# Attention by blocks of queries through all heads, with the first dense products placed between its steps

## The chip, the core and the metric

The kernel runs on one core of one Trainium2 chip. The metric is the device time of one execution in microseconds (us). The engines named below are PE (TensorE; PEld is its weight load), DVE (VectorE), ACT (ScalarE), POOL (GpSimd) and SP (SyncE), which only starts DMAs here. Each engine executes its own instructions in the order in which the program emits them, and waits at an instruction until its operands are there.

## The reference: what is computed

Two batches of 768 positions go through three stages.

1. Attention with 8 heads of 64 columns. A query sees the 96 keys up to and including itself and the first 8 keys; a slope for each head times the distance is subtracted from the score. Softmax, then the product with the values.
2. A gated unit: `h = relu(x @ w_in)` with 512 inputs and 1024 outputs, cut into `u` and `v`; `v` is normalised over its columns, multiplied over the positions with `w_spatial` (768x768), a bias is added, and the product with `u` goes through `w_out`.
3. A mixing unit: a rank-32 product over positions (`U`, `V`) is added to `x`, and then `relu(u @ w_ch1) @ w_ch2` with 2048 hidden columns is added.

## The kernel before, in words

Attention works on blocks of 128 queries. A block sees at most 232 keys (96 before it, 8 global ones, its own 128); the first block of a batch sees only 128. The heads go in pairs. A unit is one pair and one block; there are 2 batches x 4 pairs x 6 blocks = 48 units. The loop in `attention()` runs over units, all blocks of one pair before the next pair. One unit is: two score matmuls (`em_s`, 64 contraction rows each), bias and row maximum on DVE (`em_soft`), exponential and row sum on ACT (`em_exp`), a reciprocal of the sums for three units at a time on DVE (`em_sums`), the scaling on POOL (`em_norm`), transposes on PE (`em_t`) five units later, their move out of PSUM on ACT or DVE (`em_pt`), and, for three units at once, the product with the values (`em_pv`), which leaves PSUM as a rounded part and a rest (`em_x`: ACT, then DVE). The scores have four PSUM banks, the transposes two, the output two.

The dense products take every operand as such a rounded part and a rest, and use three matmuls for one product (`mm3`). The names: `m1_v` is the product with the `v` half of `w_in` (for one batch 6 tiles x 4 x 3 = 72 matmuls of 512 columns), `m2` the product with `w_spatial` (144 matmuls of 384 columns for one batch), `m1_u` that with the `u` half (96 matmuls), `m3` that with `w_out`, `m4` and `m5` those of stage 3.

Some weights come as 64-bit numbers and are decoded on the chip (`decode`: one ACT and four DVE operations for 512 columns, and then one ACT operation for the rounded part and one POOL operation for the rest). Half of `w_in` has four such pieces. They pass through a staging tile `stg` with two halves (`staged`): the third piece's DMA can start only when the first piece has left its half.

What is emitted when: `Plan` holds a model of every engine's time. Side work (decoding, loads, the normalisation of `v`) is put in as chains of operations. `tick()`, called after nearly every step, emits an operation of a chain when the model has that engine free soon enough; a chain put in while `plan.calm` is set comes after the others. `flush()` emits what is left of some chains at once, at that place of the program.

The order of the program before: attention, during whose last third the pieces of the `v` half of `w_in` are decoded as calm chains; then `m1_v` for both batches, `m2` of batch 0, `m1_u` of batch 0, `m2` of batch 1, `m1_u` of batch 1, `m3` and the rank-32 steps, and stage 3. `w_spatial` and the `u` half are decoded during `m1_v`.

The lines that set this order, from the end of `attention()` and behind it:

```
                            if p == 2:
                                plan.calm = True
                                wins = win_work(1, 0, 2048)
                ...
                flush(wins)
        ...
        for b in range(B):
            for t in range(NB):
                m1_v(b, t, bank[t % 4])
```

## Time and profile before

| | us |
|---|---|
| three runs | 552.78, 552.86, 553.55 (median 552.86) |
| the profiled execution, its time | 553.45 |
| the profiled execution, its span | 551.7 |
| busy in the span: PE / PEld / DVE / ACT / POOL | 520.7 / 450.9 / 293.8 / 217.3 / 181.0 |

Mean granted TensorE clock: 0.984 of full speed. The span is the time from the first to the last instruction. Busy time is a union over the instructions of an engine. Matmuls are pipelined and their ends are modelled, so that a start is a better mark than an end. Rows of a timeline merge neighbouring instructions of one kind: start, length, engine, line, operation, output and input, count, and in brackets the idle time before it with what ended it. All of the kernel's own instructions carry the line of one helper (L58), so the names of the tiles tell them apart: `raw` is the tile of queries, keys and probabilities, `sm` one of small numbers, `win` is `w_in`, `wsp` is `w_spatial`, `vals` the values.

### The profile page before, as it was taken

To read this page: it belongs to the slowest core of one execution; us is meant where nothing else is said; L and a number is where in the kernel's file an instruction comes from. 1 tells how busy PE (TensorE), PEld (TensorE's weight loads), DVE (VectorE), ACT (ScalarE), POOL (GpSimd) and SP (SyncE) were. 2 spreads that over 40 slices of the span, in tenths; PEclk is the share of its full clock that TensorE was granted. 3 is DMA by queue.
4 is the path that set the end of the run, shared out by engine and by line. 5 is a ranking of instruction groups with operands and counts; after the bars stand their busy time and mean duration, and the time that the engine had idled before them with its cause. 6 is when DMAs were issued, how large, how long until landed. Compare 5 with 4: busy or idle time off the path is not lost.

```text
span 551.7 us, 8005 instructions
## 1 busy us (share of the span) xinstructions
PE 520.7 (94%) x2916; PEld 450.9 (82%) x2916; DVE 293.8 (53%) x701; ACT 217.3 (39%) x527; POOL 181.0 (33%) x207
## 2 busy tenths in 40 slices
PE   5988887499999999999999999999999999999995
PEld 3656665378899999988899889889899899899894
DVE  6675656547775962379689867767122111110113
ACT  4677778355441510355453343342221221221220
POOL 2553545274471500322013432332322322323310
PEclk9999999779999999999999999999999999999998
DMA  7344331442121210232204442440003000000003
GB/s 281 120 128 150 112 130 55 163 143 87 38 78 42 76 33 0 80 131 97 74 4 135 170 154 85 145 151 2 0 3 112 1 1 1 1 0 1 1 2 120
DMA packets 9504, 42.81 MB, mean 78 GB/s; under 512 B 1264, under 2 KB 1392, under 8 KB 7408
## 3 DMA queue, kind: packets, MB, share of 16 engines
q1 hardware_dynamic: 9312, 42.21, 22.5%
q8 instruction: 25, 0.41, 0.3%
q14 instruction: 23, 0.19, 0.1%
q10 hardware_dynamic: 144, 0.00, 0.0%
HBM read 39.06 MB, written 3.15 MB: 77 GB/s over the span
## 4 chain that ended last, share of the span: by engine, by line
PE 81%; DVE 6%; ACT 6%; DMA 2%; issue 2%; POOL 2%; ACTq 0%; DVEq 0%; POOLq 0%
PE bank L58 81%; ACT raw L58 5%; DVE prob L58 3%; DVE sm L58 1%; DMA stg<-in_w_in_dram 1%; ACT x L58 1%; POOL raw L58 1%; DMA ni<-in_gl_dram 1%; DVE x L58 1%; DVE y L58 1%; DVE stg L58 1%; POOL vn L58 0%; DVE bias L58 0%; POOL win L58 0%; ACT stg L58 0%
## 5 line engine op out<-in xcount | busy, mean ns | idle before, releaser
L58 POOL TENSOR_TENSOR wch<-f,wch 128x512 fp32r<-128x512 f32 x64 | 85.7, 1359 | 213.6 <-ACT wch L58 213.6
L58 PE MATMUL bank<-x,wch 128*128 128x384 f32 x768 | 139.4, 336 | 0.0
L58 PE MATMUL bank<-wch,h 128*128 128x512 f32 x576 | 139.2, 395 | 0.0
L58 PEld LDWEIGHTS bank<-x,wch 128*128 128x128 f32 x768 | 134.7, 188 | 3.0
L58 PEld LDWEIGHTS bank<-wch,h 128*128 128x128 f32 x576 | 107.6, 188 | 23.4
L58 DVE SCALAR_TENSOR_TENSOR h<-bank,h 128x384 fp32r<-128x384 f32 x64 | 35.5, 555 | 141.6 <-ACT h L58 141.6
L58 ACT ACTIVATE h<-bank 128x384 fp32r<-128x384 f32 x64 | 31.4, 491 | 179.0 <-PE bank L58 179.0
L58 POOL TENSOR_SCALAR raw<-raw,sm 128x232 f32<-128x232 f32 (+1 forms) x96 | 43.2, 470 | 51.2 <-DVE sm L58 49.7
L58 ACT ACTIVATE raw<-prob,sm 128x232 f32<-128x232 f32 (+1 forms) x96 | 44.5, 466 | 26.2 <-DVE sm L58 17.6
L58 PE MATMUL bank<-wsp,vn 128*128 128x384 f32 x288 | 50.4, 335 | 0.4 <-ACT work L58 0.4
L58 PEld LDWEIGHTS bank<-wsp,vn 128*128 128x128 f32 x288 | 49.9, 188 | 0.8 <-ACT work L58 0.8
L58 DVE TENSOR_SCALAR f<-f 128x512 f32<-128x512 f32 (+1 forms) x64 | 40.7, 672 | 10.0 <-ACT f L58 9.7
L58 PE MATMUL bank<-win,x 128*128 128x512 f32 x144 | 37.3, 421 | 7.5 <-ACT win L58 6.9
L58 DVE SCALAR_TENSOR_TENSOR f<-raw,f 128x512 int32<-128x512 int32 x64 | 43.8, 725 | 0.1
L58 PE MATMUL bank<-raw 64*128 64x232 f32 (+1 forms) x192 | 35.6, 435 | 6.9 <-DMA raw<-in_qk_dram 5.7
L58 PEld LDWEIGHTS bank<-win,x 128*128 128x128 f32 x144 | 28.8, 203 | 15.7 <-ACT win L58 7.4
L58 PE MATMUL bank<-ident,raw 128*128 128x128 f32 (+1 forms) x176 | 30.2, 290 | 9.7 <-ACT raw L58 8.5
L58 PEld LDWEIGHTS bank<-ident,raw 128*128 128x128 f32 (+1 forms) x176 | 18.7, 140 | 24.3 <-POOL raw L58 11.9
L58 ACT ACTIVATE wch<-f 128x512 fp32r<-128x512 f32 x64 | 36.8, 624 | 1.1 <-DVE f L58 1.1
L58 PE MATMUL bank<-wo,x 128*128 128x512 f32 x144 | 35.2, 394 | 0.0
L58 PE MATMUL bank<-x,win 128*128 128x384 f32 x192 | 34.0, 336 | 0.0
L58 PEld LDWEIGHTS bank<-x,win 128*128 128x128 f32 x192 | 33.6, 188 | 0.0
(84 smaller groups left out, 505.6 us busy)
## 6 DMA issues: line engine op xcount, KB each, us to landing
raw<-in_w_ch_dram SPq DMA_DIRECT2D x16, 1024.0 KB, 4.9
vals<-in_vab_dram SPq DMA_DIRECT2D x8, 704.0 KB, 4.1
raw<-in_qk_dram SPq DMA_DIRECT2D x7, 792.0 KB, 4.5
stg<-in_w_in_dram SPq DMA_DIRECT2D x8, 512.0 KB, 4.1
out_dram<-y SPq DMA_DIRECT2D x12, 256.0 KB, 2.3
stg<-in_w_out_dram SPq DMA_DIRECT2D x4, 512.0 KB, 3.8
stg<-in_w_sp_dram SPq DMA_DIRECT2D x2, 768.0 KB, 5.3
raw<-in_qk_dram SPq DMA_DIRECT2D x2, 396.0 KB, 5.3
```

What stands on the lines that cost most here:

```text
L58: return f(*a, **kw)
```

## The change

A step g of the attention is now one block of 128 queries of one batch through all four pairs (12 blocks, `NBL`), and the host lays out queries, keys and values by block. In step g the scores of block g, the product with the values of block g-2 and the transposes of block g-1 are emitted. The four pairs' scores share four banks, two pairs side by side in each bank; softmax and exponential work in place in seven probability tiles; the sums are inverted for two pairs at a time (`em_norm`).

Between the transposes of the pairs `fill()` emits steps from a list. A step is one `mm3` of three matmuls: four steps make a tile of `m1_v` of batch 0; 48 steps are `m2` of batch 0. In steps 3 to 8 one is emitted after each pair, in steps 10 to 13 three. The transposes have two banks up to step 8 and one after that; the fillers of `m1_v` have one bank, those of `m2` two.

The `v` half of `w_in` and then `w_spatial` are put in as chains, not calm, before the first step (`early_work`). Their tiles, and those of `v` and `m2`, are no longer shared with the attention's; the attention uses other tiles in their place, among them those of the `u` half of `w_in`, whose decoding therefore is put in after the attention (`later_places`, `wu`). Then come `m1_v` of batch 1, `m1_u` of batch 0, `m2` of batch 1 and the rest as before. `U` and `V` are put in one `m1_u` later. The reciprocal root of the variance is taken with shift, negation, scaling and three Newton steps on DVE in place of a root on ACT, a reciprocal and one step.

The core of the diff (lines of the old attention that fall away are those shown above):

```diff
+            def o_load(g, e):
+                c = 0 if g % NB else C1
+                return [o_dma(raw_qk[g % 2][:, 2 * e:2 * e + 2, c:],
+                              qk[g // NB, g % NB].rearrange("p (r c) -> p r c", r=NP)[:, 2 * e:2 * e + 2, c:])]
...
+            def score(r, h):
+                return bank[r // 2 * 2 + h][:, CW * (r % 2):CW * (r % 2) + CW]
+            def prob(g, r):
+                return pb[(NP * g + r) % 7]
...
+            def em_norm(g, e):
+                r_in = rin[:, e]
+                V.tensor_scalar(out=r_in, in0=sums[:, e], scalar1=1.0e-9, scalar2=None, op0=ALU.add)
+                V.reciprocal(out=r_in, in_=r_in)
+                for r in range(2 * e, 2 * e + 2):
                     for h in range(2):
...
+                        x = prob(g, r)[:, h, c0_(g):CW]
+                        G.tensor_scalar(out=x, in0=x, scalar1=rin[:, e, r % 2, h:h + 1], scalar2=1.0,
+                                        op0=ALU.mult, op1=ALU.mult)
+            TWO = 9
+            def em_t(g, r):
+                x, bk = prob(g, r), bank[7 if g < TWO and r % 2 else 4].rearrange("p (h c q) -> p h c q", h=2, c=2)
+                c = 0 if g % NB else 1
+                if not c:
...
                 make_identity(nc, ident)
+                loads = {1: [plan.add(o_load(1, e)) for e in range(2)]}
+                pvals = {0: [], 1: [plan.add(o_vals(1))]}
+                early_work()
...
+                for g in range(NBL + 2):
+                    more = 1 if g < TWO else 3
+                    if g == NB:
+                        second_x()
+                    xs = None
+                    if g < NBL:
+                        flush(loads.get(g, []))
+                        for r in range(NP):
+                            em_s(g, r)
+                        if 0 < g and g + 1 < NBL:
+                            loads[g + 1] = [plan.add(o_load(g + 1, e)) for e in range(2)]
+                        tick()
+                    if g >= 2:
+                        flush(pvals[g - 2])
+                        em_pv(g - 2)
+                        if g < NBL:
+                            pvals[g] = [plan.add(o_vals(g))]
+                        xs = em_x(g - 2)
+                    if g < NBL:
+                        if g == 0:
+                            for h in range(2, 4):
+                                o_bias(B0, d0, m1, h)[1]()
+                        em_soft(g, 0)
+                        em_exp(g, 0)
+                    if 0 < g <= NBL:
+                        em_norm(g - 1, 1)
+                    if g < NBL:
+                        em_soft(g, 1)
+                        em_exp(g, 1)
+                        if g == 0:
+                            for h in range(4, 8):
+                                o_bias(B0, d0, m1, h)[1]()
                     if xs:
                         xs[0]()
...
+                    for r in range(NP):
+                        if xs and r == 1:
+                            xs[1]()
+                        if 0 < g <= NBL:
+                            em_t(g - 1, r)
+                            tick()
+                        fill(more)
+                        if g < NBL:
+                            if r < 2:
+                                em_soft(g, 2 + r)
+                                em_exp(g, 2 + r)
+                            if r == 1:
+                                em_norm(g, 0)
                         tick()
...
+                    if g == 0:
+                        for h in range(H):
+                            o_bias(Bt, rel, mk, h)[1]()
+                        plan.add([("V", f) for f in o_counts() + o_flag()])
+                    if 2 <= g < NB + 2:
+                        fillers.extend(s_m1_v(0, g - 2, 6))
+                    if g == TWO:
+                        fillers.extend(s_m2(0, 6))
         else:
...
+        def fill(n):
+            while n and fillers:
+                fillers.pop(0)()
+                n -= 1
...
+        def early_work():
+            win_places(1)
+            P["wv"] = win_work(1, 0, 2048)
             t_ = tl(T_SP, N_SP, "wsp")
             P["wsp"] = [t_[:, l * NB * S:(l + 1) * NB * S].rearrange("p (s t) -> p s t", s=NB) for l in range(2)]
...
+            P["vn"] = [[tl(T_VN[0][l], N_VN, f"vn0{l}").rearrange("p (t f) -> p t f", t=NB) for l in range(2)]]
             u_ = tl(T_UT, N_UT, "u")
             P["ut"] = u_.rearrange("p (k t) -> p k t", k=KB)
...
+            P["ws"] = [staged(lambda t, c=c: make(t, c)) for c in range(0, NB * S, 1536)]
+        def later_places():
+            win_places(0)
+            P["vn"].append([tl(T_VN[1][l], N_VN, f"vn1{l}").rearrange("p (t f) -> p t f", t=NB) for l in range(2)])
+            P["vw"].append([w[:, DM * n:DM * n + DM] for w in (tl(T_WK, N_WK, "work0"), tl("uv", 2 * S, "work1"))
+                            for n in range(3)])
+        def s_m1_v(b, t, k0):
+            bk = bank[k0]
+            def step(k):
+                if (b, t, k) == (0, 0, 0):
+                    flush(P["wv"])
                 mm3(bk, [X[b][l][:, k, 128 * t:128 * t + 128] for l in range(2)],
                     [win[1, l][:, k] for l in range(2)], k == 0, k == KB - 1)
...
+                if k == KB - 1:
+                    vw = P["vw"][b][t]
+                    A.activation(out=vw, in_=bk, func=AF.Relu)
+                    V.bn_stats(out=st[:, t % 2], in_=vw)
+                    V.bn_aggr(out=mv[:, b, t], in_=st[:, t % 2])
+                    if t % 3 == 2:
+                        lns[b, t // 3] = ln(b, t // 3)
+                tick()
...
+        def s_m2(b, k0):
+            def step(j, f, s, bk):
+                if (b, j, f, s) == (0, 0, 0, 0):
+                    flush(P["ws"] + [P["bs"]])
+                if j == 0 and f == 0 and s % 3 == 0:
+                    flush(lns[b, s // 3])
+                if b and j == 1 and f == 0 and s == 0:
+                    flush(gs[1])
+                c, e = 384 * j, 384 * j + 384
+                mm3(bk[:, 0:384], [P["vn"][b][l][:, s, 128 * f:128 * f + 128] for l in range(2)],
+                    [P["wsp"][l][:, s, c:e] for l in range(2)], s == 0, s == NB - 1)
+                if s == NB - 1:
+                    V.tensor_tensor(out=P["ut"][:, f, c:e], in0=bk[:, 0:384], in1=bsp[:, c:e], op=ALU.add)
+                tick()
+            return [lambda j=j, f=f, s=s: step(j, f, s, bank[k0 + f % 2 if k0 else f])
+                    for j in range(2) for f in range(KB) for s in range(NB)]
...
+        lns, gs = {}, []
+        attention()
+        later_places()
         wu = win_work(0, 0, 2048)
...
+        fill(1000)
+        for t in range(NB):
+            fillers.extend(s_m1_v(1, t, t % 4))
+        fill(1000)
         P["wo"] = [tl(f"win1{l}", 2048, f"wo{l}").rearrange("p (k f) -> p k f", k=KB) for l in range(2)]
...
                 gs.append(gated(b, j))
             if b == 0:
...
+                flush(lns[1, 0] + lns[1, 1])
+                w = tl("uv", 2 * S, "uvk")
+                upk, vpk = w[:, 0:S].rearrange("p (s r) -> p s r", s=NB), w[:, S:2 * S]
+                P["upk"], P["vpk"] = upk, vpk
+                uv = [staged(make_u), staged(lambda t: make_v(t, 0)), staged(lambda t: make_v(t, 384))]
+                fillers.extend(s_m2(1, 0))
+                fill(1000)
         P["raw"] = [tl(f"win0{l}", 2048, f"raw{l}") for l in range(2)]
         flush(gs[2] + gs[3])
         flush(w_o + uv)
```

## Rows read from the trace of the kernel before

**Rows 1.** Windows: us, busy (xcount) of PE, PEld, DVE, ACT, POOL, PEclk, DMA share, GB/s.

```profile
49.10:97.20 48.10, 41.49 (x391) 28.29 (x390) 31.14 (x144) 35.97 (x126) 24.19 (x54) 1.00 0.30 102
97.20:111.40 14.20, 6.74 (x52) 5.18 (x51) 7.63 (x14) 5.46 (x10) 4.28 (x4) 0.74 0.48 158
120.00:130.00 10.00, 10.00 (x45) 8.26 (x45) 7.72 (x17) 6.63 (x12) 5.59 (x4) 1.00 0.36 105
171.60:540.00 368.40, 368.40 (x1888) 335.21 (x1887) 179.43 (x300) 118.40 (x229) 100.33 (x76) 1.00 0.17 56
```

**Rows 2.** Timeline of PE from the attention's end to the u half's product.

```profile
101.30 1.85 PE L58 MATMUL bank<-win,x 128*128 128x512 f32 x6
110.07 0.79 PE L58 MATMUL bank<-win,x 128*128 128x512 f32 x1 [6.92 <-ACT win L58]
111.41 34.67 PE L58 MATMUL bank<-win,x 128*128 128x512 f32 x137 [0.55 <-POOL win L58]
146.48 25.26 PE L58 MATMUL bank<-wsp,vn 128*128 128x384 f32 x144 [0.40 <-ACT work L58]
171.58 16.83 PE L58 MATMUL bank<-x,win 128*128 128x384 f32 x96
```

**Rows 3.** Timeline of SP, the same columns: the third and fourth piece's DMAs.

```profile
98.72 1.65 SPq L58 DMA_DIRECT2D stg<-in_w_in_dram  x2
```

**Rows 4.** Timeline of PE within the attention, units in a row without idle time.

```profile
20.38 0.66 PE L58 MATMUL bank<-raw 64*128 64x232 f32 x4
20.98 0.64 PE L58 MATMUL bank<-ident,raw 128*104 128x128 f32 x4
21.55 1.32 PE L58 MATMUL bank<-raw,vals 128*64 128x128 f32 x20
22.80 0.66 PE L58 MATMUL bank<-raw 64*128 64x232 f32 x4
23.39 0.44 PE L58 MATMUL bank<-ident,raw 128*128 128x128 f32 x2
...
92.23 1.54 PE L58 MATMUL bank<-raw,vals 104*64 104x128 f32 x24
```

**Rows 5.** Waits from 8 to 97.2 us: us in total, times, longest.

```profile
DVE sm L58 <- ACT raw L58: 28.6, 16, 2.2
```

**Rows 6.** Timeline of DVE within the attention.

```profile
87.01 0.52 DVE L58 TENSOR_TENSOR x<-bank,x 128x384 fp32r<-128x384 f32 x1
87.44 0.39 DVE L58 CUSTOM_DVE_ANT_0 prob<-bank,bias 128x232 f32<-128x232 f32 x1
...
88.71 0.69 DVE L58 COPY raw<-bank 128x512 f32<-128x512 f32 x1
89.31 0.39 DVE L58 CUSTOM_DVE_ANT_0 prob<-bank,bias 128x232 f32<-128x232 f32 x1
```

**Rows 7.** Groups of ACT from 8 to 97.2 us: busy us, mean ns, idle before.

```profile
L58 ACT ACTIVATE raw<-prob,sm 128x232 f32<-128x232 f32 x80 | 38.2, 480 | 10.5 <-DVE sm L58 10.5
```

**Rows 8.** Groups of DVE over the whole span, the decoding in the staging tile.

```profile
L58 DVE SCALAR_TENSOR_TENSOR stg<-stg 128x512 int32<-128x512 int32 (+2 forms) x30 | 22.0, 746 | 0.2
...
L58 DVE TENSOR_SCALAR stg<-stg 128x512 f32<-128x512 f32 (+5 forms) x30 | 13.1, 460 | 4.2 <-ACT stg L58 4.1
```

**Rows 9.** Timeline of DVE at the start.

```profile
7.73 0.28 DVE L58 CUSTOM_DVE_ANT_0 prob<-bank,bias 128x128 f32<-128x128 f32 x1
...
7.94 0.70 DVE L58 SCALAR_TENSOR_TENSOR bias<-raw 128x232 f32<-128x232 f32 x2
```

**Rows 10.** Timeline of POOL: the scaling of three units, twice.

```profile
87.26 2.45 POOL L58 TENSOR_SCALAR raw<-raw,sm 128x128 f32<-128x128 f32 x6 [2.72 <-DVE sm L58]
92.71 3.90 POOL L58 TENSOR_SCALAR raw<-raw,sm 128x232 f32<-128x232 f32 x6 [3.00 <-DVE sm L58]
```

**Rows 11.** DMA issues: KB each, median us to landing.

```profile
raw<-in_qk_dram SPq DMA_DIRECT2D x7, 792.0 KB, 4.5
stg<-in_w_in_dram SPq DMA_DIRECT2D x8, 512.0 KB, 4.1
```

More of the change, by code (lines that the diff above doesn't have):

```diff
@@ L26 @@
 CW = C1 + 128
-KST = 128 + GS
-KXW = NB * KST
-VP = 22 * D
-QKW = KST + 128
+QKW = CW + 128
+NBL = B * NB
 NCH = 16
@@ L368, in stt @@
+            t_ = tl("x10", KB * S, "masks")
+            rel, mk = (t_[:, k * CW:(k + 1) * CW] for k in range(2))
+            iot = t_[:, 512:512 + CW + 128].bitcast(I32)
+            ps0, r0, d0, m1 = (t_[:, 1024 + 128 * k:1152 + 128 * k] for k in range(4))
             def stt(o_, i0, sc, i1, op0, op1):
@@ new lines, in em_soft, with em_exp @@
+            def em_soft(g, r):
+                c0, bt = c0_(g), Bt if g % NB else B0
+                for h in range(2):
+                    V.tensor_tensor_reduce(out=prob(g, r)[:, h, c0:CW], in0=score(r, h)[:, c0:CW], in1=bt[:, 2 * r + h],
+                                           scale=-0.125, scalar=3.0e38, op0=ALU.add, op1=ALU.min,
+                                           accum_out=mneg[:, (NP * g + r) % 8, h:h + 1])
+            def em_exp(g, r):
+                for h in range(2):
+                    x = prob(g, r)[:, h, c0_(g):CW]
+                    A.activation(out=x, in_=x, func=AF.Exp, scale=-1.0, bias=mneg[:, (NP * g + r) % 8, h:h + 1],
+                                 accum_out=sums[:, r // 2, r % 2, h:h + 1])
@@ new lines, in body @@
+            TWO = 9
+            def em_t(g, r):
+                x, bk = prob(g, r), bank[7 if g < TWO and r % 2 else 4].rearrange("p (h c q) -> p h c q", h=2, c=2)
+                c = 0 if g % NB else 1
+                if not c:
+                    for h in range(2):
+                        T.transpose(bk[0:C1, h, 0], x[:, h, 0:C1], ident)
+                for h in range(2):
+                    T.transpose(bk[:, h, 1], x[:, h, C1:CW], ident)
+                if r % 2:
+                    V.tensor_copy(ptb[r][:, :, c:], bk[:, :, c:])
@@ L484, in em_pt @@
                 else:
[L485 removed]
+                    A.activation(out=ptb[r][:, :, c:], in_=bk[:, :, c:], func=AF.Copy)
             def em_pv(g):
[L489 to L493 removed]
+                for r in range(NP):
+                    for c in range(0 if g % NB else 1, 2):
+                        k = (C1, 128)[c]
@@ L494, in em_pv @@
                         for h in range(2):
-                            T.matmul(bank[5 + g % 2][64 * h:64 * h + 64, 128 * (u % 3):128 * (u % 3) + 128], w[0:k, n, h],
-                                     ptb[u % 6][0:k, h, c], start=c == 0 or not i, stop=c == 1)
+                            T.matmul(bank[5][64 * h:64 * h + 64, 128 * r:128 * r + 128], vt[g % 2][0:k, r, c, h],
+                                     ptb[r][0:k, h, c], start=c == 0 or g % NB == 0, stop=c == 1)
             def em_x(g):
-                b, pr, i = units[3 * g]
@@ L567, in attention @@
-                flush(wins)
-                return lambda: None, []
+                    for r in range(NP):
+                        if xs and r == 1:
[10 more added lines that the diff above has]
+                                em_norm(g, 0)
+                        tick()
@@ L643, in attention @@
                                 sub(V, lo, bank[5][:, 0:128], hi)
-                flush(win_work(1, 0, 2048))
-                return lambda: None, []
-        P = {}
+                early_work()
+                for b in range(1):
+                    for t in range(NB):
+                        fillers.extend(s_m1_v(0, t, 6))
+                fillers.extend(s_m2(0, 6))
+        P = {}
+        fillers = []
+        def fill(n):
+            while n and fillers:
+                fillers.pop(0)()
+                n -= 1
         mv = sm[:, 96:96 + 24].rearrange("p (b t s) -> p b t s", b=2, t=6)
@@ new lines, in step @@
+                tick()
+            return [lambda k=k: step(k) for k in range(KB)]
+        def s_m2(b, k0):
[14 more added lines that the diff above has]
+                    for j in range(2) for f in range(KB) for s in range(NB)]
@@ L873, in body @@
             if b == 0:
-                for j in range(2):
-                    for f in range(KB):
-                        if j == 1 and f == 0:
-                            flush(gs[1])
-                        m2(1, f, j, bank[f])
-                        tick()
+                flush(lns[1, 0] + lns[1, 1])
[5 more added lines that the diff above has]
+                fill(1000)
         P["raw"] = [tl(f"win0{l}", 2048, f"raw{l}") for l in range(2)]
```

279 lines of the change are left out of this document (62 added, 217 removed).

## The prediction

> **What bounds the kernel now.** I read the page's slices first: PE is busy throughout but for the start, the tail and a hole at 97 to 111 us. Then the windows: behind 171.6 us PE is busy for 368.4 of 368.4 us [rows 1], so nothing that the change does there can gain; all of it is decided before that point. The timeline of PE then shows the stretch piece by piece [rows 2]: the attention ends at 101.3 us, six matmuls of `m1_v` run, PE waits 6.92 us for the decoded `w_in`, and the 144 matmuls of `m1_v` end at 146.48 us. They have taken 45.2 us. At the rate of a warm stretch, 45 in 10 us [rows 1], they take 144 x 0.222 = 32.0 us. So 13.2 us are lost there: the wait, and a clock granted at 0.74 in that window. The wait's cause is on SP [rows 3]: the third and fourth piece's DMAs start at 98.72 us, since the decoding before them was held back.
>
> Within the attention I take PE's price from starts [rows 4]: a unit's scores 0.60 us (20.38 to 20.98), its transposes 0.57, and 20 instructions of the value product 1.25, so 32 of them (four units) 2.0. Four units cost 4 x 0.60 + 4 x 0.57 + 2.0 = 6.68 us. The pace is slower: from the value product at 21.55 to that at 92.23 us lie 13 groups of three units, 5.44 us each, 7.25 us for four units. The difference, 0.57 us, is a loop of waits: DVE stands 28.6 us in 16 waits for ACT's last sum of three units [rows 5], and softmax of the next unit is queued behind that wait. So the attention is nearly full on PE already; what it has to spare is small, and what can be won is above all the 13.2 us behind it.
>
> **The change part by part.** I call the twelve blocks of the new loop steps, and sum until PE can start `m1_u` of batch 0, which was 171.58 us [rows 2].
>
> *Steps 0 to 2, no fillers.* The wait for the mask numbers stays, so DVE reaches its first softmax at 7.5 us as before. Step 0 then holds on DVE 8 softmax operations at 0.21 us (7.73 to 7.94), 6 short biases (not seen singly; between 0.21 and 0.35, I take 0.25) and 8 long ones at 0.35 [rows 9], and one inversion of sums (two short operations, estimated at 0.4 together): 1.7 + 1.5 + 2.8 + 0.4, so 13.9 us. Before, most of the biases came between later units; here they stand in front of step 1. Steps 1 and 2 hold 16 softmax operations at 0.32 (87.44 to 88.71 for four), four moves out of PSUM, two of them half as wide, at 0.60 and 0.35, a rest of 512 columns (0.43 for 384, so 0.57) [rows 6], four inversions at 0.4, and 7 short operations for the flag, 2.0: 5.1 + 1.9 + 0.6 + 1.6 + 2.0 = 11.2. Into these steps falls the decoding of `w_in`, 4 pieces of 2 x 0.746 + 2 x 0.460 = 2.41 us [rows 8], 9.6 us. If DVE does all of it one after the other, step 3 starts at 13.9 + 11.2 + 9.6 = 34.7 us; if the decoding slips into DVE's waits, at 13.9 + 2 x 7.25 = 28.4. I take 34.7, since DVE's own work alone is 5.6 of the 7.25 us of a step.
>
> *Steps 3 to 8* carry one filler after each pair: 12 matmuls x 0.222 = 2.67 us. On PE 6 x (6.68 + 2.67) = 56.1, less what block 6, the first of a batch, saves: 4 transposes shorter by 0.2 (0.44 against 0.64 [rows 4]), half of its value product, 1.0, and by its columns (128 of 232) some 1.1 of scores: 53.2 us. Beside it ACT has 8 exponentials at 0.48 [rows 7] and three moves, no more than 0.60 each by the move on DVE [rows 6], 5.6 us, and DVE 8 x 0.32 + 2 x 0.60 + 0.57 + 0.8 = 5.1 us. New on DVE in steps 3 to 9: three rests of `w_spatial`, six statistics and six normalisations of 512 columns, at 0.60 by the move of that size, and some 30 short operations at 0.21 (Newton's among them): 9.0 + 6.3 = 15.3 us, 2.2 a step. 7.3 of 9.3 us are taken then: PE stays the longest.
>
> *Step 9* has no filler: 7.25 us. *Steps 10 to 13* hold 8 units' scores (4.8), 12 units' transposes (6.8), four value products (8.0) and the 144 matmuls of `m2`, 25.1 as before (146.48 to 171.58): 44.7 us. The one transpose bank must be moved out before the next transposes; three fillers stand between them, 9 x 0.174 = 1.57 us, against a move of 0.60. *`m1_v` of batch 1*: 72 x 0.222 = 16.0.
>
> The sum: 34.7 + 53.2 + 7.25 + 44.7 + 16.0 = 155.9 us.
>
> *Waits added.* In order, a filler stands before the next pair's transposes, and those before the moves on ACT and DVE, behind which softmax and exponentials of the later pairs are queued. The order helps too: an inversion now stands behind two later softmax operations, so that DVE needn't stand still for ACT. Between no wait at all (0) and the loop of before with the fillers on top (0.57 a step), I take the upper end, since no row shows such a mix: 8 steps, 4.6 us.
>
> *The `u` half of `w_in`* is decoded only behind the attention. Its staging is free by then, so two of its pieces are loaded; DVE needs 9.6 us for the four and 6 x 0.8 for the statistics of `m1_v`, inside 16.0 us, but the last two pieces wait for a half of the staging tile and a DMA of 4.1 us [rows 11]. It costs between 0 and the 6.92 us that the same decoding cost before [rows 2]; a gain is excluded, as PE can't pass it. I take 1.5.
>
> *DMAs.* A step issues two loads of queries and keys, together 128 x 4 x 360 x 4 bytes = 720 KB, and one of values, a step ahead; 792 KB took 4.5 us to land [rows 11], a step lasts 7 to 9. SP is in order: behind a staging DMA that waits for its half, the next step's loads wait too, which costs nothing until it exceeds some 3 us. The half of the loads needed first is smaller than before (256 of 360 columns), and the mask numbers come later than it anyway: nothing. The Newton steps, the later `U` and `V`, the other tiles: nothing, with `m1_u` and `m2` of batch 1, over 40 us on PE, as their cover.
>
> So PE starts `m1_u` at 155.9 + 4.6 + 1.5 = 162.0 instead of 171.6 us: 9.6 us earlier, and what follows is unchanged. From the profiled execution's 553.45 us (its span 551.7 and 1.75 around it) that gives 543.9. It lies 0.6 above the median of the three runs, 552.86, to which a new measurement is compared: 543.3, so 543 us.
>
> **Two rules weighed.** Six scalings on POOL took 2.45 us in a quiet group and 3.90 us beside decoding on DVE [rows 10]. The Trainium skill (SBUF — State Buffer, section Who interferes with whom) says why: POOL shares a pair of SBUF ports with DVE, and the one that starts second waits for the whole instruction of the other. This speaks against the change, which puts decoding beside every step; by that rule a step's eight scalings cost 5.2 instead of 3.3 us, which the sum holds at nothing, since a step lasts over 9 us, and which would be 1.9 a step on the path.
>
> In the attention's window PE is busy for 41.49 of 48.1 us, its weight loads for 28.29; behind 171.6 us the weight loads are busy for 91% [rows 1]. The Trainium skill (Perfetto Trace Analysis, section Identifying the Most-Contended Engine) holds the busy share of matmuls for no measure of what is left and takes that of the weight loads; by that rule a third of the attention would be free for fillers. The starts say otherwise: 6.68 of 7.25 us.
>
> **The rivals.** *All hides* (537, down to 531). Without the 4.6 and the 1.5 the sum is 155.9, a gain of 15.7: 537; with the decoding in DVE's waits too, 149.6: 531. For it: four independent pairs in a step, and inversions off the loop. Against: DVE and PE both near full in steps 3 to 8.
>
> *Fillers are free* (515). If PE had a third to spare, steps 3 to 8 would last 7.25 instead of 9.9 us and steps 10 and 11 would lose their 6.3: 16 + 12.6 below 162.0, a gain of 38. Against it stand the starts.
>
> *The new work lengthens the loop* (548 to 559, the other side). The 15.3 us that are new on DVE in steps 3 to 9 stand in the queue before softmax or a move for which PE waits; a scaling held up on POOL does the same for the transposes. If all of it is on the path: 162.0 + 15.3 = 177.3, slower by 5.7: 559; a half: 551. It decides from 9.6 of the 15.3, a mean step of 9.9 + 1.4 = 11.3 us. For it: 28.6 us of such a wait in the loop of before. Against: DVE has 2 us a step left.
>
> *The decoding comes too late* (559). If the planner holds the chains back, the first filler's flush puts all four pieces before the rest of step 3: 4.8 us for two, then the 12.7 us from the last pieces' DMAs to PE's restart, as before (98.72 to 111.41) [rows 2, 3], and the slow clock behind it (137 matmuls in 34.67 instead of 30.4 us, 4.3), less 6.3 that steps 1 and 2 save: 15.5 more, 177.5, slower by 5.9. Against: the chains aren't calm and the staging is free from the start.
>
> **How the numbers follow.** Forecast 0.45 (its own range 539 to 547); all hides 0.22; fillers free 0.03; the longer loop 0.15; decoding too late 0.15. Range 531 to 557: it leaves out the free fillers, most of the late decoding and the ends of the others, some 0.2. About 0.2% (1.1 us) is what a measurement of this kernel can tell from no change. Faster: 0.45 + 0.22 + 0.03 + 0.09 of the longer loop = 0.79; the same 0.04; slower 0.17.
>
> **What would show it.** Right: no PE idle time of several us with `win` as releaser; step 3 at 30 to 35 us; starts of value products 9.3 to 10.5 us apart in steps 3 to 8; `m1_u` at 158 to 166 us, the same 380 us behind it, and a granted clock of 1.00 at 100 to 120 us. Wrong: steps of over 11 us with PE waiting for DVE or POOL; a stretch in which DVE does nothing but decode while PE stands; or an idle stretch ahead of `m1_u`.

## The result, and the profile after

| | before | after |
|---|---|---|
| runs of the first comparison, us | 552.67 to 553.55 (4), median 552.82 | 544.98 to 548.58 (4), median 546.55 |
| ratio, 95% interval | | 0.9886 (0.9844 to 0.9928) |
| the profiled execution: time, span | 553.45, 551.7 | 547.89, 546.1 |
| mean granted clock of it | 0.984 | 0.973 |

The kernel is 6.3 us faster; forecast were 9.8 (543.0; range 531 to 557). Timed again in six runs beside ten of before, the ratio is the same, 0.9886 (0.9855 to 0.9917). Its own ten runs spread over 4.9 us (544.98 to 549.89).

I read the timeline of PE first. The kernel after, from step 3 to the `m1_u` of batch 1; a step starts at its row of scores, `bank<-raw` (columns as in [rows 2]):

```profile
30.83 0.49 PE L56 MATMUL bank<-win,x 128*128 128x512 f32 x1 [2.24 <-ACT win L56]
...
39.87 0.80 PE L56 MATMUL bank<-win,x 128*128 128x512 f32 x1 [4.00 <-ACT win L56]
...
44.51 2.26 PE L56 MATMUL bank<-raw 64*128 64x232 f32 x16
...
53.30 1.84 PE L56 MATMUL bank<-raw 64*128 64x232 f32 x16
55.06 1.98 PE L56 MATMUL bank<-ptb,vals 104*64 104x128 f32 x32
56.97 0.65 PE L56 MATMUL bank<-ident,prob 128*104 128x128 f32 x4
57.37 0.94 PE L56 MATMUL bank<-win,x 128*128 128x512 f32 x3
58.15 0.60 PE L56 MATMUL bank<-ident,prob 128*104 128x128 f32 x4
...
61.68 1.16 PE L56 MATMUL bank<-raw 64*128 64x128 f32 x16
...
71.44 0.62 PE L56 MATMUL bank<-ident,prob 128*104 128x128 f32 x4 [3.16 <-DVE ptb L56]
...
72.69 3.46 PE L56 MATMUL bank<-raw 64*128 64x232 f32 x16
...
89.39 1.84 PE L56 MATMUL bank<-raw 64*128 64x232 f32 x16
...
97.50 1.07 PE L56 MATMUL bank<-ident,prob 128*104 128x128 f32 x4 [2.32 <-DVE ptb L56]
98.50 3.47 PE L56 MATMUL bank<-raw 64*128 64x232 f32 x16
...
144.61 16.52 PE L56 MATMUL bank<-win,x 128*128 128x512 f32 x72
160.97 2.08 PE L56 MATMUL bank<-x,win 128*128 128x384 f32 x11
...
183.57 9.81 PE L56 MATMUL bank<-wsp,vn 128*128 128x384 f32 x55 [0.88 <-POOL vn L56]
194.63 12.75 PE L56 MATMUL bank<-wsp,vn 128*128 128x384 f32 x72 [1.26 <-DVE u L56]
207.22 16.80 PE L56 MATMUL bank<-x,win 128*128 128x384 f32 x96
```

Three things stand in it. Step 3 holds two waits for the rounded part of `win`, which ACT writes (2.24 and 4.00 us), and two shorter ones for the rest, from POOL (0.86 and 0.56; not shown), 7.66 us in all. Steps 4 and 5 are full: from 44.51 to 61.68 PE never waits. Steps 6 and 9 each end in a wait for a move on DVE, with the scores behind it at half their rate (3.46 against 1.84 us). And the last rows hold what the forecast did not: behind `m1_u`, where [rows 1] had no idle time, PE waits four times (two are shown; the others are 0.65 us for `win` and 0.63 for `vn`). In the kernel before the `m1_u` of batch 1 starts here:

```profile
213.23 17.12 PE L58 MATMUL bank<-x,win 128*128 128x384 f32 x96
```

From `m1_u` of batch 0 to that of batch 1 took 213.23 - 171.58 = 41.65 us before and 207.22 - 160.97 = 46.25 after: of 10.6 us gained, 4.6 are given back. What lies behind is unchanged (551.7 - 213.23 = 338.5; 546.1 - 207.22 = 338.9).

Windows of the kernel after (columns of [rows 1]):

```profile
30.00:50.00 20.00, 13.75 (x81) 10.22 (x82) 11.37 (x41) 10.21 (x28) 9.23 (x14) 0.74 0.60 208
...
100.00:110.00 10.00, 10.00 (x80) 9.03 (x77) 5.69 (x24) 5.91 (x18) 6.21 (x9) 0.83 0.18 53
...
170.00:180.00 10.00, 10.00 (x60) 10.00 (x59) 9.96 (x17) 5.33 (x10) 6.55 (x5) 1.00 0.19 56
180.00:190.00 10.00, 8.49 (x47) 7.68 (x46) 10.00 (x14) 4.73 (x11) 5.54 (x5) 1.00 0.10 29
```

The clock is the first reading: 0.74 around step 3's waits, 0.83 behind the wait of step 9. The second is DVE: 19.96 of 20 us from 170 to 190. There it decodes `w_out`, normalises batch 1's `v`, and gates. PE's four waits behind `m1_u` are for the last piece of the `u` half (0.65 us), twice for the normalised `v` (0.63 and 0.88), and for DVE's move of `m2`'s own sums out of PSUM (1.26). `w_out` was decoded beside `m1_u` before the change too; what is new beside it is batch 1's normalisation. In the kernel before that was done under `m2` of batch 0, and ended ahead of `m1_u` (171.58). Timeline of POOL in the kernel before, the last normalised tiles and the first piece of `w_out`:

```profile
162.53 3.83 POOL L58 TENSOR_TENSOR vn<-work,vn 128x512 fp32r<-128x512 f32 x3 [1.03 <-ACT vn L58]
176.14 1.29 POOL L58 TENSOR_TENSOR wo<-stg,wo 128x512 fp32r<-128x512 f32 x1 [9.79 <-issue]
```

Not all of the 19.96 us is DVE's own work. Operations that fall together with POOL's subtractions take longer than their like, as these two of one form show (timelines of DVE and of POOL in the kernel after):

```profile
174.98 0.42 DVE L56 TENSOR_SCALAR stg<-stg 128x512 f32<-128x512 f32 x1
182.31 1.49 DVE L56 TENSOR_SCALAR stg<-stg 128x512 f32<-128x512 f32 x1
```

```profile
179.08 4.43 POOL L56 TENSOR_TENSOR vn<-work,vn 128x512 fp32r<-128x512 f32 x3 [1.03 <-ACT vn L56]
```

Added up row by row against rows of the same kind elsewhere, some 8 of the 20 us are such lengthening (an estimate from DVE's timeline). No run takes it away.

What answers to [rows 3]: the SP queue still starts the third and fourth piece's DMAs late, and DVE then stands idle in the midst of the decoding, behind which the next softmax (`CUSTOM_DVE_ANT_0`) is queued. Timelines of SP and of DVE:

```profile
28.48 1.86 SPq L56 DMA_DIRECT2D stg<-in_w_in_dram  x2
```

```profile
33.87 0.43 DVE L56 TENSOR_SCALAR stg<-stg 128x512 f32<-128x512 f32 x1 [3.87 <-ACT stg L56]
36.25 1.10 DVE L56 TENSOR_SCALAR stg<-stg 128x512 f32<-128x512 f32 x3 [1.95 <-ACT stg L56]
...
39.67 0.39 DVE L56 CUSTOM_DVE_ANT_0 prob<-bank,bias 128x232 f32<-128x232 f32 x1
```

What makes step 6 wait: the chain of Newton steps and two normalisations on DVE, 64.45 to 69.6 us, with softmax and the move that PE needs (`ptb`, 70.62) behind it. Timelines of DVE and of POOL:

```profile
64.45 1.21 DVE L56 TENSOR_SCALAR sm<-sm 128x3 f32<-128x3 f32 x3
...
66.31 0.36 DVE L56 SCALAR_TENSOR_TENSOR sm<-sm 128x3 f32<-128x3 f32 x2
...
66.90 1.35 DVE L56 SCALAR_TENSOR_TENSOR sm<-sm 128x3 f32<-128x3 f32 x2
...
68.68 1.00 DVE L56 TENSOR_SCALAR u<-u,sm 128x512 f32<-128x512 f32 x2
...
70.62 0.68 DVE L56 COPY ptb<-bank 128x512 f32<-128x512 f32 x1
```

```profile
66.94 1.28 POOL L56 TENSOR_TENSOR wsp<-stg,wsp 128x512 fp32r<-128x512 f32 x1 [0.87 <-ACT wsp L56]
```

The wait of [rows 5] is gone: from 8 to 97.2 us the list of waits holds no wait of DVE for ACT's sums; ACT now waits for DVE, as its first line shows (total, times, longest):

```profile
ACT prob L56 <- DVE sm L56: 17.0, 14, 3.1
```

In the group that answers to [rows 10] a scaling takes 0.51 us in the mean, so eight take 4.1 us, between the two prices weighed in the prediction (3.3 and 5.2).

```profile
L56 POOL TENSOR_SCALAR prob<-prob,sm 128x232 f32<-128x232 f32 (+1 forms) x96 | 47.0, 509 | 50.5 <-ACT prob L56 21.5
```

A piece of `w_in` lands in 5.1 us (the median of eight), against 4.1 in [rows 11].

### The profile page after: what moved, and what is told of

Same layout as the page of the kernel before. It is cut to its first block, busy times and chain, and to the rows that moved or that the text cites. A ratio compares the mean times of both kernels' runs of the same rounds, so it can differ in the third digit from the quotient of the medians.

```text
span 546.1 us, 7966 instructions
## 1 busy us (share of the span) xinstructions
PE 511.6 (94%) x2916; PEld 452.9 (83%) x2916; DVE 305.0 (56%) x745; ACT 212.6 (39%) x510; POOL 183.0 (34%) x207
## 4 chain that ended last, share of the span: by engine, by line
PE 78%; DVE 16%; ACT 2%; DMA 2%; issue 1%; POOL 0%; ACTq 0%; POOLq 0%; DVEq 0%; SPq 0%
PE bank L56 78%; DVE sm L56 4%; DVE stg L56 3%; DVE prob L56 3%; DVE x L56 1%; DVE work L56 1%; DVE u L56 1%; DMA stg<-in_w_in_dram 1%; DVE ptb L56 1%; DVE y L56 1%; DVE bias L56 1%; ACT prob L56 1%; DMA ni<-in_gl_dram 1%; ACT ptb L56 0%; ACT u L56 0%
## 5 line engine op out<-in xcount | busy, mean ns | idle before, releaser
L56 POOL TENSOR_SCALAR prob<-prob,sm 128x232 f32<-128x232 f32 (+1 forms) x96 | 47.0, 509 | 50.5 <-ACT prob L56 21.5
L56 PE MATMUL bank<-wsp,vn 128*128 128x384 f32 x288 | 54.4, 341 | 2.8 <-POOL vn L56 1.5
L56 ACT ACTIVATE prob<-prob,sm 128x232 f32<-128x232 f32 (+1 forms) x96 | 44.4, 464 | 31.9 <-DVE sm L56 31.7
L56 PE MATMUL bank<-win,x 128*128 128x512 f32 x144 | 42.2, 427 | 7.7 <-ACT win L56 6.2
L56 PE MATMUL bank<-ident,prob 128*128 128x128 f32 (+1 forms) x176 | 29.3, 291 | 10.7 <-DVE ptb L56 5.5
L56 PEld LDWEIGHTS bank<-ident,prob 128*128 128x128 f32 (+1 forms) x176 | 21.4, 143 | 19.0 <-issue 8.9
L56 PEld LDWEIGHTS bank<-win,x 128*128 128x128 f32 x144 | 26.5, 199 | 12.8 <-ACT win L56 6.7
L56 PE MATMUL bank<-raw 64*128 64x232 f32 (+1 forms) x192 | 28.8, 454 | 5.5 <-DMA raw<-in_qk_dram 5.0
```

Of the source, the lines that this page charges most:

```text
L56: return f(*a, **kw)
```

## The experiments

Ratios are to the kernel before on the same chip, with 95% intervals; "earlier" is against the trace of the kernel after.

**Where the 4.6 us behind `m1_u` go.** `w_out`'s decoding is put in one `m1_u` later.

```diff
-        w_o = weights64(w_out, flat(P["wo"][0]), flat(P["wo"][1]), 2048)
         flush(wu)
...
+                w_o = weights64(w_out, flat(P["wo"][0]), flat(P["wo"][1]), 2048)
                 uv = [staged(make_u), staged(lambda t: make_v(t, 0)), staged(lambda t: make_v(t, 384))]
```

> The decoding of w_out is put in behind m1_u of batch 0 instead of ahead of it. Theory (in m1_u of batch 0 DVE has the u half's decoding, the root and normalisation of batch 1 and the decoding of w_out at once, so that m2 of batch 1 waits for normalised tiles): the stretch from the start of m1_u of batch 0 to that of m1_u of batch 1 falls from 46.3 to 42 us or a little more, the time by 3 to 5 us to 541 to 544. Rival (the waits come from the u half's decoding and the normalisation alone, or w_out now comes too late for its product): 45 us or more there, or a new wait ahead of the product with w_out, 545 to 549.

Measured: 541.55 us, 0.9795 (0.9777 to 0.9813). Its timeline of PE:

```profile
159.35 2.08 PE L56 MATMUL bank<-x,win 128*128 128x384 f32 x11
...
176.92 25.13 PE L56 MATMUL bank<-wsp,vn 128*128 128x384 f32 x144
201.88 16.80 PE L56 MATMUL bank<-x,win 128*128 128x384 f32 x96
```

The 144 matmuls run without a wait, and the stretch takes 201.88 - 159.35 = 42.5 us instead of 46.25, 3.7 of the 5.0 us that the time gains; the rest lies ahead of `m1_u`, which starts 1.6 us earlier. The planner had put the decoding of a weight that is needed at 224 us in front of and in between the operations of a normalisation that is needed at 180. Of the three edits tried singly it gains the most.

**Step 3's waits.** The last two pieces of `w_in` get a staging place of their own (the tile of `u`, unused then), so that their DMAs wait for nothing.

```diff
-            P["wv"] = win_work(1, 0, 2048)
+            P["wv"] = [staged(lambda t: piece(t, 0)), staged(lambda t: piece(t, 512)),
+                       plan.add(piece(u_[:, 0:1536], 1024)), plan.add(piece(u_[:, 1536:3072], 1536))]
```

> The third and fourth piece of the v half of w_in get staging places of their own (in the tile u, free until step 3 ends), so that all four DMAs can start at once. Theory (two pieces wait for the staging halves, and the flush puts that wait in front of step 3 on DVE): PE's idle time at the win pieces, 7.7 us between 28 and 42 us in the changed kernel, falls below 3 us, the slow clock behind it goes, m1_u of batch 0 starts 5 to 9 us earlier (152 to 156 instead of 161.0), and the time is 538 to 542. Rival (DVE is full in steps 0 to 3, the pieces wait for DVE and not for the DMA): PE still waits 5 us or more there, the time stays at 545 to 548.

Measured: 543.78, 0.9828 (0.9809 to 0.9847), between the two expected ranges; `m1_v` of batch 1 starts 3.4 us earlier. One wait for `win` of 1.62 us is left of 7.66, but 3.69 us for a move appear in step 2, since the decoding now stands there on DVE. So the late DMAs were half of it; the other half is DVE's own load, which the sum had held.

```profile
25.64 0.62 PE L56 MATMUL bank<-ident,prob 128*104 128x128 f32 x4 [3.69 <-ACT ptb L56]
...
36.37 0.72 PE L56 MATMUL bank<-win,x 128*128 128x512 f32 x2 [1.62 <-POOL win L56]
```

**Steps 6 and 9.** Both normalisations of batch 0 may emit at most one operation of a chain per call of `tick()`.

```diff
                 key = c.ops[0][0]
+                if c in done:
+                    continue
...
                     self.emit(c)
                     more = True
+                    if c.slow:
+                        done.append(c)
```

> The normalisation chains of batch 0 (the root by Newton steps and its application) are emitted at most one operation at each planner call instead of in a lump. Theory (a lump of 12 to 15 operations stands ahead of softmax and of a move out of PSUM, for which PE waits): PE's idle times of 3.2 us at 68 to 71 us and of 2.3 us at 95 to 97 us fall below 1 us each, the slow clock behind both goes, and the time is 540 to 544. Rival (DVE's total work is the bound of these steps): the same idle time shows up spread over steps 6 to 9, the time stays at 545 to 548.

Measured: 544.99, 0.9851 (0.983 to 0.9872), an interval that overlaps with the kernel after. The waits of 3.16 and 2.32 us are gone, and scores run at full rate in steps 6 to 10; but `vn` is late for the fourth step of `m2` (three waits, 3.4 us; the longest):

```profile
100.29 0.62 PE L56 MATMUL bank<-wsp,vn 128*128 128x384 f32 x2 [2.17 <-ACT vn L56]
```

**The Newton steps undone.** The root is taken on ACT again, with one short DVE operation ahead of it and five behind it.

```diff
-                ("V", lambda: V.tensor_scalar(out=r.bitcast(I32), in0=e.bitcast(I32), scalar1=1, scalar2=-1,
-                                              op0=ALU.logical_shift_right, op1=ALU.bitwise_xor)),
...
+                ("A", lambda: A.activation(out=q_, in_=e, func=AF.Sqrt)),
+                ("V", lambda: V.reciprocal(out=r, in_=q_)),
```

> One part undone: the reciprocal root of the variance is again a root on ACT, a reciprocal and one step on DVE (5 short DVE operations in place of 12 in a chain). Theory A: it was the length of the DVE chain that put PE's 3.16 us wait in step 6 and the 2.32 us wait in step 9; both fall under 1.5 us, and 'm1_v' of batch 1 starts 2 to 4 us before 144.6. The root's table on ACT has to be loaded and the exponential's loaded back, 1.28 us each time, and that costs 1 to 2 us of it: 543 to 546 us. Rival B: the three normalisations behind the chain and the POOL operations beside it make the lump, so the waits stay, and the tables come on top with some 2.6 us for each of the two roots inside the attention, in front of exponentials: 549 to 552 us.

Measured: 550.14, 0.9955 (0.9938 to 0.9973), rival B's number. The short chain doesn't spare the waits: they come one step later (2.13 us for a move on ACT and 1.01 for one on DVE, at 76 to 78 us; 2.07 at 104 us). Since the table loads came with the short chain, this run can't tell which of the two they belong to. ACT loads tables six times instead of once, 1.28 us each; the group's line in this kernel:

```profile
L56 ACT ACT_TABLE_LOAD x6 | 7.7, 1283 | 2.1 <-PEq L1006 1.2 <-DVE sm L56 0.8
```

So the Newton steps, which I held at nothing, gain some 3.8 us against the root on ACT with its table loads (0.9955 - 0.9886, the intervals apart), though it is their chain behind which PE waits in step 6.

**How much of the fillers is hidden.** None at all: `m1_v` and `m2` of batch 0 behind the attention (each through the PSUM banks it had as a filler).

```diff
-                        fill(more)
...
-                    if g == TWO:
-                        fillers.extend(s_m2(0, 6))
```

> The changed kernel without any filler: m1_v and m2 of batch 0 come behind the attention, all else as changed. Theory (in undisturbed steps PE needs 5.2 us for the attention's own work, 1.76 for scores, 1.91 for values and 4 x 0.38 for transposes, and the step without fillers lasts about 7; so fillers save about 2 us in each of 8 steps, unless what they wait for gives it back): attention steps of 6.8 to 7.5 us, no stall at step 3, m1_u of batch 0 at 150 to 158 us; against 161.0 in the changed kernel that is a time of 537 to 545, so that the fillers as placed bring nothing. Rival (the fillers carry the gain): m1_u later than 163, time 549 or more.

Measured: 569.74, 1.0311 (1.0284 to 1.0338): 23 us slower than the kernel after, and my expectation missed. Rows of its steps 4, 5 and 9:

```profile
32.74 2.80 PE L56 MATMUL bank<-raw 64*128 64x232 f32 x16
...
49.10 1.07 PE L56 MATMUL bank<-ident,prob 128*104 128x128 f32 x4 [2.97 <-DVE ptb L56]
...
71.87 3.12 PE L56 MATMUL bank<-raw 64*128 64x232 f32 x16
```

Steps 4 to 8 last 71.87 - 32.74 = 39.1 us without fillers and 89.39 - 44.51 = 44.9 with them: 60 matmuls, 13.3 us at the warm rate, cost 5.8. Without fillers PE stands idle for 8.1 of the 39.1 us (31.02 busy), close to the other 7.5. A wait of 2.97 us for a move on DVE stands there as well. Part of the 23 us is the experiment's own: `m1_v` of batch 0 behind the attention has one PSUM bank and waits 0.69 us for each tile, `m2` waits for `vn`.

Only `m2` is put behind the attention; steps 3 to 8 keep theirs.

```diff
-                    if g == TWO:
-                        fillers.extend(s_m2(0, 6))
```

> The changed kernel with the m1_v fillers kept and the m2 fillers taken out: m2 of batch 0 comes behind the attention in one piece. Theory (steps 10 and 11 without fillers last about 7 us against a PE load of 5.2, so m2 as filler saves 2 x 2 us less its own waits of about 1.3): m1_v of batch 1 starts 1 to 4 us later than 144.6, time 547 to 550. Rival (m2 as filler is worth nothing): the start at 141 to 144.6, time 543 to 546.5.

Measured: 556.58, 1.0069 (1.0052 to 1.0087), slower than I expected; the execution of the rows below took 560.89. The transposes of block 8, in step 9, are the last with two banks. With one bank and nothing between them PE waits some 3 us in step 10, and as long in step 11:

```profile
107.22 0.62 PE L56 MATMUL bank<-ident,prob 128*104 128x128 f32 x4 [0.84 <-ACT ptb L56]
108.78 0.62 PE L56 MATMUL bank<-ident,prob 128*104 128x128 f32 x4 [0.94 <-DVE ptb L56]
110.71 0.62 PE L56 MATMUL bank<-ident,prob 128*104 128x128 f32 x4 [1.32 <-POOL prob L56]
```

`m2` among the steps is thus worth some 10 us here (0.0183 of 552.7), in part because the second transpose bank was given up for it: in the run without any filler PE waits 0.40 us among the transposes of step 9, with two banks, and 3.2 in step 10, with one.

**The hole alone, in the old loop.** First, the decoding is put in earlier and not as a calm chain.

```diff
+                            if p == NP - 1:
+                                flush([counted])
+                                wins = win_work(1, 0, 2048)
...
-                                plan.calm = True
-                                wins = win_work(1, 0, 2048)
```

> The kernel before, with one thing changed: the decoding of the v half of w_in is put in at the 18th unit and not as calm chains (for this the flag's operations are emitted at that place too). No interleaving, no new order. Theory (the gain of the change is the hole behind the attention, 13.2 us, less what it gives away): the wait of 6.9 us and the slow clock behind the attention go, 9.6 us of DVE work move into the attention, and the time is 540 to 546, as fast as the changed kernel. Rival (the interleaving of products and attention is what pays): the attention becomes longer by as much as the hole was, 550 to 554.

Measured: 557.47, 1.0077 (1.0055 to 1.0098), and no answer: the model of engine times held the chains back to 98 us all the same, and the hole stayed (6.94 us). The attention also ended 3.5 us later (`m1_v` at 104.83 instead of 101.30), which no run explains. Then each operation by hand, at most one DMA and one other operation a unit from the 20th on:

```diff
+                    if v == 18:
+                        wins = win_work(1, 0, 2048)
+                    if v > 18:
+                        force()
```

> The kernel before, with the decoding of the v half of w_in (and ahead of it the flag's operations) emitted by hand, one operation for each unit from the 19th unit on, so that the planner can't hold it back as it did with the early chains. No interleaving, no new order. Theory (the old order has waits enough on DVE for this decoding, and the hole behind the attention is all that it costs): no PE idle time over 1 us and a granted clock of 1.00 behind the attention, the attention at most 4 us longer, 541 to 545. Rival (the old loop of waits has no room: each forced operation lengthens it by its own time): the attention ends 8 us later or more, 548 to 553.

Measured: 548.58, 0.9933 (0.9913 to 0.9952), granted clock 0.996 in the profiled execution, no hole:

```profile
108.03 33.42 PE L58 MATMUL bank<-win,x 128*128 128x512 f32 x144
141.28 25.15 PE L58 MATMUL bank<-wsp,vn 128*128 128x384 f32 x144
```

`m2` starts 5.2 us earlier than in [rows 2], not 13.2: `m1_v` starts 6.7 us later, so the decoding lengthens the old loop, as the rival had it, if by less than its 8 us. Filling the hole is worth some 4 us in the old order.

**The version that beats both.** The staging of the first edit, the spreading for the first normalisation alone, and `w_out` later.

```diff
+                c_.slow = (b, g) == (0, 0)
```

> The three mends together: own staging places for two pieces of w_in, the first normalisation chain of batch 0 spread (the second as a lump, since m2 waited for it when both were spread), w_out's decoding behind m1_u of batch 0. If the three losses are separate places, their gains add: 2.8 + 1.5 + 5.0 below 546.6, so 536 to 539. If DVE's total is what counts, they overlap: 540 to 542.

Measured: 536.12, 0.9702 (0.9684 to 0.9721), granted clock 0.992 in the profiled execution. `m1_u` starts 8 us earlier than in the kernel after, and the 144 matmuls behind it run unbroken; its timeline of PE:

```profile
152.90 2.08 PE L56 MATMUL bank<-x,win 128*128 128x384 f32 x11
...
170.49 25.13 PE L56 MATMUL bank<-wsp,vn 128*128 128x384 f32 x144
```

The second normalisation spread too, three operations of a chain per call:

> The combined version of before (two w_in pieces staged in another tile, the first normalisation of batch 0 spread to one operation of a chain per call of the planner, w_out decoded behind m1_u of batch 0) with the second normalisation spread as well, three operations of a chain at a time. If the lump of DVE operations at 85.6 to 88.4 us is what makes PE wait 2.33 us at 90.55 and run the scores behind it at half clock, both go, some 2 us: 533.5 to 535.5 against 536.1. Rival: the normalised v then comes late for the fourth step of m2, as it did with one operation at a time, PE waits there for vn, and it is 536 to 538.

Measured: 535.41, 0.9682 (0.9655 to 0.9709), not told apart from the last: the 2.33 us wait is gone, and three waits of some 0.4 us for `vn` and one of 0.78 for a move have come in its place.

The changed kernel again, and the combined version without the spreading:

> The changed kernel itself, timed again in more runs, since its ratio so far (0.9886, 0.9844 to 0.9928) overlaps with those of the two small edits (0.9828 and 0.9851). If the small edits gained what their traces show (3.4 and 2.6 us at the start of m1_v of batch 1), it lies at 546 to 548 us, a ratio of 0.988 to 0.991. Rival: it lies at 544 to 545.5, a ratio under 0.987, as its two fastest runs did, and then the edits' gains are within what one kernel's runs differ by.

> Two of the three edits of the combined version: two w_in pieces staged in another tile, and w_out decoded behind m1_u of batch 0; the first normalisation is not spread. If the three gains add up, this one lacks the 2.6 us of the spreading: 538 to 539.5 us, with a wait of some 3 us for a DVE move in step 6 and scores at half clock behind it. Rival: the wait was only moved (the spread version has its own waits later), and the time is that of the combined version, 535.5 to 537.

Measured: 545.79 (ratio given above), between the two expected ranges, and 540.26, 0.9776 (0.9753 to 0.9799), slower than either expectation. By these times the spreading is worth 540.26 - 536.12 = 4.1 us, more than the 2.6 by which `m1_v` of batch 1 started earlier in its own run, where the second chain had come late. The two profiled executions show 2.4 us at that start (138.91 and 136.54); the first of them, 538.53 us, was the fastest of its kernel. The staging is told apart from the kernel after by itself (0.9809 to 0.9847 against 0.9855 to 0.9917), but not on top of `w_out` (0.9795 to 0.9776).

## Why the prediction was right, and where its steps failed

| starts, us of the span | forecast | after |
|---|---|---|
| step 3 | 34.7 | 24.27 |
| step 4 | 34.7 + 9.35 = 44.1 | 44.51 |
| step 9 | 34.7 + 53.2 = 87.9 | 89.39 |
| step 10 | 95.2 | 98.50 |
| `m1_v` of batch 1 | 139.9 | 144.61 |
| `m1_u` of batch 0 | 155.9 + 6.1 = 162.0 | 160.97 |
| `m1_u` of batch 1 | 162.0 + 41.65 = 203.7 | 207.22 |

The rows above `m1_u` are the forecast's sums without the 6.1 us that it added for waits. The time came out in good part by luck: errors of single steps cancel, as shown below. What held is that the decoding is paid for ahead of step 4, that filled steps run at PE's rate where nothing waits (steps 4 and 5), and that the waits before `m1_u` amount to about what was allowed, in other places.

*Steps 0 to 3.* The 9.6 us of decoding were summed into steps 0 to 2; most came in step 3. At step 4 forecast and trace agree within 0.5 us, by chance: step 3 started 10.4 us early and took 20.2 instead of 9.35. In it DVE stood idle for 5.8 us (3.87 and 1.95) behind the late DMAs, which the sum did not have. The mechanism was that of the rival "the decoding comes too late": the flush at the first filler put pieces three and four, with their DMAs, in front of softmax. Its price was not: with steps 1 and 2 as quick as they were, the 7.66 us of waits cost nothing against my sum.

*Steps 4 to 8.* PE's price of an undisturbed step was too high: scores 1.76 us (53.30 to 55.06), values 1.91, four transposes at some 0.38: 5.2 us, not the 6.68 worked out from [rows 4]. There the groups of matmuls are shorter, and from 20.38 to 22.80 PE's weight loads stand idle for 0.17 to 0.29 us ahead of each; whether these are waits or the price of small groups, no run tells. A filler's price was too low, 0.78 instead of 0.67. With four of them an undisturbed step is 8.3, and the step from 53.30 took 8.38, not 9.35. By the new loop's price PE had 2.0 of the old 7.25 us to spare, 28%. Here the rule of the Trainium skill (Perfetto Trace Analysis, section Identifying the Most-Contended Engine), against which I argued, pointed the right way: the share of weight loads left a third free. Step 6 took the difference back: a wait of 3.16 us, and 1.6 more for the scores behind it at half clock. So steps 4 to 8 took 44.9 us against 43.9, again by chance.

*Steps 9 to 13.* Step 9 took 9.1 us instead of 7.25, with the wait of 2.32 us for the second chain, and the rest 46.1 instead of 44.7, the first 5 us or so of step 10 at the lower clock (0.50 granted from 98.5 to 101.5 us, 0.68 from 101.5 to 104.5). The chain's twelve short operations were held at 0.21 us each, 2.5 us, and DVE was to have "2 us a step left". In step 6 they took 4.2 (64.45 to 68.68), in one piece, in front of the move that PE waited for. A mean per step doesn't see whether a load comes in one lump.

*Behind `m1_u`* stands the failed step: "nothing, with `m1_u` and `m2` of batch 1, over 40 us on PE, as their cover", and "what follows is unchanged". The cover was PE's time; what ran out was DVE's, busy for 19.96 of 20 us from 170 to 190. With `m2` of batch 0 gone into the attention, batch 1's normalisation no longer has it as cover; it met beside `m1_u` with the gating and with `w_out`'s decoding, which the planner emitted in between. These 4.6 us, less the 1.0 that `m1_u` came ahead of the forecast, are most of the 4.0 by which the profiled executions miss it (553.45 - 547.89 = 5.6, not 9.6). `w_out` put in later takes 3.7 of the 4.6 back (first experiment).

*POOL beside DVE.* The prediction weighed this at POOL's scalings alone, and held it at nothing. Its two rows differ in form: a quiet group of 128x232 took 2.62 us (at 81.92), not 2.45, so 1.3 of its 1.45 us remain. What the sum lacked is the other side, DVE's operations held up beside POOL's subtractions: Newton's steps in step 6 (1.35 us for two), and by the estimate above some 8 us from 170 to 190, in the stretch that fails the forecast. How much of the 4.6 us that makes was not tested.

*The rivals.* "All hides" fails by step 3, 6 and 9; "fillers are free" holds for about half of their price; the longer loop is seen in two steps of the seven from 3 to 9, not all. Of the signs I named, `m1_u` at 158 to 166 us held. Five failed: step 3 at 24.27 us instead of 30 to 35; a wait for `win` of 4.00 us; value products 20.7 us apart across step 3 and then 7.5 to 13.3, instead of 9.3 to 10.5; a clock of 0.83, not 1.00, at 100 to 110 us; 385.1 us behind the start of `m1_u`, not 380. One sign of being wrong came too: step 6 lasted 11.0 us, with PE waiting for DVE. The time alone would have hidden all of these.

Left open: how the gain splits between the hole filled and the fillers hidden in the new loop. The runs without fillers carry costs of their own, and the old loop without a hole is another loop.

## What to carry to other kernels

Where work moves from one stage to another, add up each engine's time in the stage that receives it, DVE's above all: a stretch where the bottleneck engine is 100% busy is a cover only as long as the others keep up. Side work that a planner emits wherever an engine is free wants an order by when it is needed: a weight needed 40 us later went in between a normalisation needed at once, and moving one line gained 5 us. Where an engine reads as full, see whether its operations are longer than their like: part of that time can be another engine's doing. And fillers between dependent steps hid 7.5 of their 13.3 us here, about the idle time that the same steps show without them.

## What was not expected of the hardware

Two short DVE operations of three columns, 0.36 us for a pair elsewhere in the chain, took 1.35 us at 66.90 and ended with POOL's subtraction (66.94, 1.28 us). The Trainium skill (SBUF — State Buffer, section Who interferes with whom) says that a DVE instruction with two SBUF inputs contends with a POOL instruction that reads SBUF; the row agrees, and shows that size is no protection. From 167 to 176 us three more such rows stand beside POOL's subtractions (1.25 us for two, 0.79 and 1.25 for one, where one takes 0.15 alone).

Waits of 2 to 4 us were followed by scores at half rate in some executions and not in others of the same program: behind the 2.32 us wait of step 9 they took 3.47 us in one execution of the kernel after and 1.84 in the next, the start of `m1_v` of batch 1 moving from 144.61 to 143.74. The second execution's rows:

```profile
97.78 0.62 PE L56 MATMUL bank<-ident,prob 128*104 128x128 f32 x4 [2.32 <-DVE ptb L56]
98.33 1.84 PE L56 MATMUL bank<-raw 64*128 64x232 f32 x16
```

The mean granted clock of the ten runs of the kernel after goes with their times (0.972 at 548.58 and 549.89 us, 0.98 at 544.98, 545.2 and 545.45; one exception, 0.975 at 545.49). That fewer such waits make for less spread is not shown: the combined version spreads over 0.7 us (535.97 to 536.69), but the one with both normalisations spread, and fewer waits, over 2.0, and the one with only `w_out` moved, which keeps them all, over 1.5.
